# A convolution-attention and MLP-mixer kernel on one core: the order of its prologue, the queue that fetches the weights, and how chunk 0 enters the main loop

## The chip, the cores and the metric

The kernel runs on one core of a Trainium2 chip. The metric is the time of one execution on the device in microseconds (us), the median of several runs. The engines of the core work in parallel and meet at semaphores: TensorE (PE, with its weight load PEld), VectorE (DVE), ScalarE (ACT), GpSimd (POOL) and SyncE (SP). DMAs are issued by SP, ACT or GpSimd and are carried out by 16 DMA engines which the core's queues share.

## The reference

x is [8, 4096, 192], the weight generator [8, 4096, 8, 7] (both float32); the four MLP weights come as 64-bit floats. Cut to what matters:

```python
w = softmax(weight_gen, axis=-1)               # 7 taps for each of 8 heads
x = sum over k of w[..., k] * x[s - 6 + k]     # causal convolution attention
xt = x.transpose(0, 2, 1)
h = np.maximum(xt @ w_tok1, 0.0) @ w_tok2      # tokens mixed: 4096 -> 256 -> 4096
u = x + h.transpose(0, 2, 1)
h2 = np.maximum(u @ w_ch1, 0.0) @ w_ch2        # channels mixed: 192 -> 1536 -> 192
return (u + h2).astype(np.float32)
```

## The kernel before, in words

The 8 x 4096 tokens are cut into 64 chunks of 512, eight to a batch. Since w_tok1 sums over all tokens of a batch, the attention of a whole batch has to be done before the first u of that batch. Products run with two-part operands (hi and lo, fp32r), so that each product costs two or three passes.

**Prologue** (lines 914 to 1034, pools `pro` and `ps_pro`). It makes the attention of batch 0's eight chunks in 16 half chunks i: DVE multiplies the taps (`product`, L356, into `prk`, three buffers), PE adds the seven taps by 21 transposes into `tapsum` (`sums`, L362), ACT copies the sum out (`keep_sum`, L378, "the eviction"), PE turns it back (`turn_back`), ACT copies that (`keep_turned`, L393, into `xa`), and PE adds the half chunk's share of x w_tok1 into `th` (`token1_half`, L957, one half behind). Beside it the 64-bit weights are turned into float32 (`convert`, L151): each raw tile of 1024 or 768 pairs takes three ACT steps (L168, L171, L172) and one DVE step (L167). Eight such tiles are w_tok1 (`tok`), one is w_tok2's first (`w2`), three are w_ch1's thirds (`w1`), and after them comes w_ch2's first third (`c2`). The tables `loads`, `steps` and `after` say at which i a load is issued, which ACT steps stand ahead of that i's eviction (up to three), and which DVE step is put in. All loads and the stores `s0` of converted w_tok1 (`store_val`, L961) are issued by SP; only the stores `xs` of attended chunks are issued by GpSimd. Three buffers `raw` hold fetched weights, five `val` in `pro` hold converted w_tok1 until it has been stored.

**Into the main loop.** `make_h1` relus `th` into `h1`. Tiles of the pool `late` (`uf`, `u_hi`, `u_lo`, `h` and others) take the memory of `pro`. For chunk 0, `token2` makes h1 w_tok2 in PSUM (`acc`, L571), six more products (L1051) run on PE, DVE adds x into `uf` (L583, L584), and `u_parts` writes u_hi and u_lo by eight ACT casts and two DVE steps. Two rows of batch 1's first softmax stand ahead of that on DVE (L199, L200).

**Main loop, chunk g** (from L1131). `channel1(g, p)`, p = 0..5: 18 products u w_ch1 into `ph` (L637; three PSUM buffers). `take_h`: ACT relu (L643) and DVE rest (L644) into `h` (four buffers). `channel2(g, p)`: ten products h w_ch2 into `acc` (L655), and behind p = 2 the ten products of the next chunk's u (`token2`, L571, into `up`, which ACT first fills with x, L563 or L565). Everything else (conversions left over, the attention of later batches, output copies) is put between by the planner `pump`, which keeps a modelled time for each engine. In chunk 0 it has to place w_ch2's second third ahead of p = 2, its last third ahead of p = 4, and w_tok2's second tile ahead of chunk 1's u.

## Time and profile before

| | |
|---|---|
| median of 3 runs | 2085.78 us (2084.53 to 2088.27) |
| the profiled execution | 2085.23 us, of which the span of the profile is 2083.5 us |
| PE busy | 2041.8 us, 98% of the span |
| DVE, ACT, POOL busy | 1501.5, 1435.4 and 163.3 us |
| granted clock of PE, mean | 0.996 of full speed |

The profile is of one execution. Times in it are counted from the start of the span. A row of a timeline gives the idle time ahead of it and what ended it; that name is inferred from semaphores, and where a wait has several semaphores it may be another one.

### The profile page before, as it was taken

What the parts mean: (1) busy time and instruction counts of PE and PEld (TensorE: products, weight loads), DVE (VectorE), ACT (ScalarE), POOL (GpSimd) and SP (SyncE); (2) the same over time, 40 slices, a digit from 0 to 9 for tenths busy, and PEclk for the clock granted to TensorE, in tenths of its full rate; (3) what the DMA queues carried; (4) which work ended last, traced back from release to release, by engine and by line L of the source; (5) the groups of instructions that cost most, each with busy time, mean ns of one, the idle gap of its engine ahead of it and who ended that gap; (6) DMA issues with size and microseconds to landing.
All of it is one profiled execution on the core that took longest, in us unless ns stands there. A gap on an engine that the chain in (4) does not pass through costs nothing.

```text
span 2083.5 us, 32275 instructions
## 1 busy us (share of the span) xinstructions
PE 2041.8 (98%) x12832; PEld 1679.5 (81%) x12832; DVE 1501.5 (72%) x1724; ACT 1435.4 (69%) x2221; POOL 163.3 (8%) x200
## 2 busy tenths in 40 slices
PE   7799999999999999999999999999999999999998
PEld 6678888888887888888888888888888888888887
DVE  8779887888887777777777778677677765343343
ACT  6678765677766766766766766766676676676665
POOL 0000111111111000111000011010011100000000
PEclk9999999999999999999999999999999999999999
DMA  9947668788777667666656766566766654322121
GB/s 356 315 155 237 175 186 235 188 231 234 201 207 216 178 173 204 180 186 168 169 172 198 207 168 190 160 174 180 206 179 182 168 162 116 91 72 63 48 60 24
DMA packets 169815, 365.41 MB, mean 175 GB/s; under 512 B 16840, under 2 KB 110792, under 8 KB 154304
## 3 DMA queue, kind: packets, MB, share of 16 engines
q1 hardware_dynamic: 143680, 285.74, 42.6%
q0 software_dynamic: 25984, 77.61, 18.8%
q8 instruction: 101, 1.65, 0.3%
q14 instruction: 50, 0.41, 0.1%
HBM read 225.92 MB, written 71.30 MB: 143 GB/s over the span
## 4 chain that ended last, share of the span: by engine, by line
PE 78%; DVE 3%; DMA 1%; ACT 0%; issue 0%; ACTq 0%; SPq 0%; DVEq 0%
PE acc L655 35%; PE ph L637 31%; PE up L571 7%; PE th L531 4%; PE th L533 2%; DVE h L644 1%; DVE pr L231 1%; PE acc L672 0%; DMA out_dram<-out_tile 0%; DVE pr L245 0%; DMA xt<-in_x_dram 0%; ACT up L565 0%; DVE oc L712 0%; DVE xa L231 0%; DVE oa L709 0%
## 5 line engine op out<-in xcount | busy, mean ns | idle before, releaser
L655 PE MATMUL acc<-h,w2s 128*128 128x512 f32 x3800 | 886.1, 390 | 2.0 <-DVE w2s L494 2.0
L655 PEld LDWEIGHTS acc<-h,w2s 128*128 128x128 f32 x3800 | 710.4, 188 | 148.6 <-DVE w2s L494 2.4
L643 ACT ACTIVATE h<-ph 128x1024 fp32r<-128x1024 f32 x384 | 394.6, 1028 | 348.7 <-PE ph L637 302.5
L644 DVE SCALAR_TENSOR_TENSOR h<-ph,h 128x1024 fp32r<-128x1024 f32 x384 | 468.3, 1220 | 120.8 <-ACT h L643 120.1
L637 PE MATMUL ph<-u_hi,w_hi 64*128 64x512 f32 x2304 | 339.5, 395 | 7.9 <-ACT u_hi L607 4.8
L637 PE MATMUL ph<-u_lo,w_hi 64*128 64x512 f32 x2304 | 331.1, 388 | 0.6 <-ACT u_lo L612 0.3
L637 PE MATMUL ph<-u_hi,w_lo 64*128 64x512 f32 x2304 | 329.2, 387 | 0.0
L231 DVE TENSOR_TENSOR pr<-xt,wg 128x768 f32<-128x768 f32 x336 | 311.7, 947 | 0.2
L637 PEld LDWEIGHTS ph<-u_hi,w_hi 64*128 64x128 f32 x2304 | 215.1, 185 | 74.5 <-issue 19.4
L637 PEld LDWEIGHTS ph<-u_lo,w_hi 64*128 64x128 f32 x2304 | 219.9, 184 | 48.5 <-ACT u_lo L613 0.9
L637 PEld LDWEIGHTS ph<-u_hi,w_lo 64*128 64x128 f32 x2304 | 219.3, 184 | 46.9
L249 POOL DMA_DIRECT2D xa<-pr x168 | 146.5, 872 | 1408.2 <-DVE pr L245 843.6
L719 ACT COPY out_tile<-oa 32x256 f32<-32x256 f32 x504 | 203.5, 404 | 8.0
L584 DVE TENSOR_TENSOR uf<-up,uf 64x512 f32<-64x512 f32 x63 | 43.0, 683 | 211.9 <-ACT uf L579 211.9
L245 DVE TENSOR_TENSOR pr<-pr 128x768 f32<-128x768 f32 x168 | 160.2, 954 | 3.5
L571 PE MATMUL up<-w,h 128*128 128x512 f32 x630 | 160.9, 401 | 1.6 <-ACT up L565 1.2
L571 PEld LDWEIGHTS up<-w,h 128*128 128x128 f32 x630 | 114.2, 188 | 42.8 <-issue 13.4
L531 PE MATMUL th<-xh,w 128*128 128x384 f32 x384 | 112.5, 358 | 0.0
L290 DVE TENSOR_TENSOR xh<-xa,xh 128x768 fp32r<-128x768 f32 x48 | 45.8, 954 | 91.4 <-ACT xh L287 91.3
L719 ACT COPY out_tile<-oc 32x256 f32<-32x256 f32 x252 | 101.6, 403 | 7.6 <-DVE oc L712 3.1
L565 ACT COPY up<-xb 128x1024 f32<-128x1024 f32 x56 | 57.0, 1017 | 67.2 <-DVE h L644 65.8
L533 PE MATMUL th<-xh,w 128*128 128x192 f32 x384 | 96.2, 250 | 0.0
(89 smaller groups left out, 1636.4 us busy)
## 6 DMA issues: line engine op xcount, KB each, us to landing
w<-s SPq DMA_DIRECT2D x96, 1024.0 KB, 5.9
xa<-pr POOLq DMA_DIRECT2D x168, 384.0 KB, 5.0
xt<-in_x_dram SPq DMA_DIRECT2D x56, 960.0 KB, 8.1
out_dram<-out_tile SPq DMA_DIRECT2D x128, 192.0 KB, 4.7
xb<-xs SPq DMA_DIRECT2D x368, 64.0 KB, 5.3
xs<-t SPq DMA_DIRECT2D x56, 384.0 KB, 4.9
raw<-in_moe_w_tok_dram SPq DMA_DIRECT2D x16, 1024.0 KB, 12.7
s<-w POOLq DMA_DIRECT2D x8, 1024.0 KB, 5.9
```

The lines of the kernel that those rows point to most:

```text
L231: nc.vector.tensor_mul(t.rearrange("p t (h g) -> p (t h) g", h=H).rearrange("p (o n) g -> p o n g", o=1), x_k, w)
L245: nc.vector.tensor_add(sums[m], sums[m], prt.pop(m))
L249: nc.gpsimd.dma_start(xat[m].rearrange("p t d -> p (t d)"), sums[m].rearrange("p t d -> p (t d)"), accum_op=ALU.add)
L531: nc.tensor.matmul(th[:, r, 0:2 * D], w[:, c, 0, rs], xh[:, c, :], start=i + c == 0, stop=False, skip_group_check=True)
L533: nc.tensor.matmul(th[:, r, 0:D], w[:, c, 1, rs], xh[:, c, 0:D], start=False, stop=c == CT - 1, skip_group_check=True)
L565: nc.scalar.copy(up.rearrange("p k (n b c) -> p (k n) c b", c=CT, b=Q), xb.rearrange("p k (n c b) -> p (k n) c b", c=CT, b=Q))
L571: nc.tensor.matmul(up[:, n, :], h1[:, k, d], w[:, l, k * N:(k + 1) * N], start=k == 0 and j == 0 and not seeded, stop=k == KR - 1 and j == ...
L637: nc.tensor.matmul(ph[:, j, :], w[rows, k, p * P:(p + 1) * P], u[rows, k], start=n == 0, stop=n == len(steps) - 1)
L643: nc.scalar.activation(h[:, :, 0, :], ph, AF.Relu)
L644: nc.vector.scalar_tensor_tensor(h[:, :, 1, :], ph, 0.0, h[:, :, 0, :].bitcast(F32), op0=ALU.max, op1=ALU.subtract)
L655: nc.tensor.matmul(acc[:, n, :], w2s[:, f, d], h[:, j, l, :], start=False, stop=f == NF - 1 and i == len(steps) - 1, skip_group_check=True)
L719: nc.scalar.copy(dst, src[to:to + Q].rearrange("p (n e d) -> p n e d", n=2, d=Q)[:, n])
```

## The change

- **Queues.** Inside the prologue the weights are fetched by GpSimd, and `store_val` is issued by GpSimd too. SP keeps x, `xs` reads and the weight generator, whose first pair of loads goes to ACT's queue. x of chunk 0 is issued first; the two memsets of `xb` on GpSimd move behind the identity.
- **First softmax in halves.** `softmax` takes the chunks it does; chunk 0's half stands ahead of the first product and chunk 1's between the first products.
- **Order of the conversions.** Instead of `steps` there are `before` (at most two ACT steps ahead of an eviction) and `behind` (one step behind it), each starting one or two halves later; `halves` puts `token1_half` of i = 0 at 2 and of 1 and 2 at 3. The rest of w_ch1's conversion goes behind the loop. w_ch2's first and second thirds are fetched in the prologue and converted in the main loop, as is all of batch 1's softmax; the loads of batch 1's x go into the table.
- **Chunk 0's u.** PSUM tile `up` (pool `ps_acc`) is opened by eight transposes of the identity, ACT writes x into it (`seed_up`), `first_token2` adds the products, and u is split straight from PSUM (`first_u`: seven ACT and five DVE instructions). The same tile is then `acc` of chunk 0, without `seed` (a copy, L700). Two more products stand in for the six.
- **Chunk 0's first products.** `first_channel1` does p = 0 and 1 together, sorted by the third k of u's rows: for each k first the products with u_hi, then those with u_lo.
- **Planner.** `jobs` and `soon` hold the moved conversions, w_ch2's first third is asked for ahead of p = 0, and the modelled times at the start differ.

```diff
-        if pro is not None and n % 3 == 0:
+        if pro is not None and n % 3 == 0 and tag is None:
...
-        nc.sync.dma_start(
+        nc.gpsimd.dma_start(
             raw[:, 0:CT * R, :].rearrange("p n l -> p (n l)"),
...
-        nc.sync.dma_start(
+        (nc.sync if pro is None else nc.gpsimd).dma_start(
             raw[:, 0:KR * N, :].rearrange("p (k n) l -> p k (n l)", k=KR),
...
+        queue = nc.sync if pro is None else nc.gpsimd
...
+    def first_u(up):
...
+        act(hi[:, 0], up[:, 0])
+        act(hi[c, 1], up[e, 0])
+        act(hi[e, 1], up[c, 0])
+        dve.tensor_sub(lo[:, 0], up[:, 0], hi[:, 0].bitcast(F32))
+        dve.tensor_copy(uc[c], up[e, 1])
+        dve.tensor_add(uc[c], up[c, 1], uc[c])
+        act(hi[c, 2], uc[c])
+        dve.tensor_copy(hi[e, 2], uc[c])
+        act(lo[c, 1], f[e, 0])
+        act(lo[e, 1], f[c, 0])
+        dve.tensor_sub(lo[c, 2], uc[c], hi[c, 2].bitcast(F32))
+        act(lo[e, 2], f[c, 2])
+        ut[0] = hi, lo
...
+    def first_channel1(ps):
...
+        for k in range(3):
+            for steps in (((w1_hi, u_hi), (w1_lo, u_hi)), ((w1_hi, u_lo),)):
+                for p in ps:
+                    for w, u in steps:
+                        for j in range(2):
...
+        load_x(0)
+        load_wg(0, nc.scalar)
...
         def store_val(m):
-            nc.sync.dma_start(s0[m], vals[m][0])
+            nc.gpsimd.dma_start(s0[m], vals[m][0])
...
-        run(soft[0])
...
+        run(islice(soft[0], 7))
...
+        dve(w2)
+        act(w2)
+        rest(w1[0])
+        dve(w1[1])
         keep_turned(i)
+        act(w1[1])
         dve(w2)
         rest(w2)
+        dve(w1[1])
+        rest(w1[1])
+        seed_up(0, up, xbt.pop(0))
         token1_half(i)
-        rest(w1[1])
-        load_pair(NCH)
+        dve(w1[2])
...
-        rest(c2)
-        soft = softmaxes()
-        run(islice(soft, 2, 4))
...
+    first_token2(up)
+    acc_t[0] = up
+    first_u(up)
...
-            if g == 0 and p % (NP // 3) == 0 and p > 0:
+            if g == 0 and p % (NP // 3) == 0:
```

Three places of the order follow; the names are tiles, a number behind one tells buffers apart, and the line numbers of the change are its own.

GpSimd at the end of the prologue, before: the last attended chunks go out, then the store of w_tok2's first tile, the pad rows of batch 1's x, and the clearing of `uf`.

```order
L398 DMA xs5_656<-sum_603 128x768
L398 DMA xs6_755<-sum_696 128x768
L398 DMA xs7_848<-sum_789 128x768
L453 DMA s3_77<-w2_858 128x2048
L93 MEMSET xt_869 2x1152
L1045 MEMSET uf_908 64x512
```

The same place in the change: L475 fetches w_ch2's thirds, L1010 stores converted w_tok1 (`s0`) out of `val`.

```order
L398 DMA xs6_785<-sum_727 128x768
L92 MEMSET xt_787 2x1152
L475 DMA raw_793<-in_moe_w_ch2_dram 128x4x384
L1010 DMA s0_76<-val_391 128x1024
L475 DMA raw_836<-in_moe_w_ch2_dram 128x4x384
L1010 DMA s0_76<-val_438 128x1024
L398 DMA xs7_874<-sum_825 128x768
L1010 DMA s0_76<-val_570 128x1024
L1010 DMA s0_76<-val_619 128x1024
L1010 DMA s0_76<-val_724 128x1024
L453 DMA s3_78<-w2_882 128x2048
L1116 MEMSET uf_915 64x512
```

What moved: five stores out of `pro`'s `val` tiles, which SP issued before, stand on GpSimd behind fetches, and the last three of them behind the last attended chunk `xs7`.

ACT from the end of the loop to the first cast of chunk 0's u, before, with what each waits for (DMAHW is a DMA of SP's or ACT's queue, DMASW one of GpSimd's).

```order
L393 COPY xa<-turn 128x384 [waits PE_49]
L186 CAST w_858<-val 128x1024 [waits DVE_49]
L186 CAST w_hi<-val 128x3x256 [waits DVE_49]
L508 ACTIVATE h_877<-th 128x2x192 [waits PE_49]
L186 CAST w_hi<-val 128x3x256 [waits DVE_49]
L168 ACTIVATE few<-raw 128x768 [waits DMAHW3_49,DMASW5_49]
L171 ACTIVATE few<-raw 128x768 [waits Activation_49]
L172 ACTIVATE val<-raw 128x768
L493 CAST w2s<-val 128x4x192 [waits DVE_49]
L607 CAST u_hi<-uf 128x512 [waits DMAHW2_49,DMAHW3_49,DMAHW0_49,DMAHW4_49,DVE_49,Activation_49]
```

The same place in the change.

```order
L378 COPY sum<-tapsum 128x384 [waits PE_49]
L185 CAST w_882<-val 128x1024 [waits DVE_49]
L393 COPY xa<-turn 128x384 [waits PE_49]
L185 CAST w_hi<-val 128x3x256 [waits DVE_49]
L577 COPY acc<-xb_74 128x2x4x128 [waits DMAHW5_49,DMAHW6_49,DMAHW4_49,DMAHW7_49,DMAHW3_49,Pool_49]
L509 ACTIVATE h_900<-th 128x2x192 [waits PE_49]
L185 CAST w_hi<-val 128x3x256 [waits DVE_49]
L601 CAST u_hi<-acc 128x512 [waits DMASW4_49,DMASW3_49,DMASW6_49,DMASW2_49,DMAHW0_49,DMASW0_49,DMAHW1_49,PE_49,Activation_49]
L602 CAST u_hi<-acc 64x512
L603 CAST u_hi<-acc 64x512
```

What moved: the relu into h1 (L508, now L509) stands behind one w_ch1 cast as before, w_ch2's third (L168 to L493) is gone from here, x is written into PSUM ahead of the relu, and the first cast of u waits for five semaphores of GpSimd's queue, which are those of the last five stores into `s0`.

ACT in chunk 0, before, from the third relu to the filling of chunk 1's `up` with x (L563); `raw_852` is w_tok2's second tile.

```order
L643 ACTIVATE h_1027<-ph_1008 128x2x512
L700 COPY acc_1030<-uf_908 128x1024
L643 ACTIVATE h_1051<-ph_1032 128x2x512
L493 CAST w2s_70<-val_954 128x4x192
L168 ACTIVATE few_1007<-raw_852 128x1024
L172 ACTIVATE val_1006<-raw_852 128x1024
L643 ACTIVATE h_1112<-ph_1054 128x2x512
L186 CAST w2_1111<-val_1006 128x1024
L563 COPY up_1130<-xb1_72 128x2x4x128
```

In the change, from the cast of w_ch2's first third (L494) to the same filling (L577); `raw_836` is w_ch2's second third, `raw_1082` w_tok2's second tile, `raw_1117` w_ch2's last third.

```order
L494 CAST w2s_73<-val_950 128x4x192
L167 ACTIVATE few_1088<-raw_836 128x768
L171 ACTIVATE val_1087<-raw_836 128x768
L686 ACTIVATE h_1103<-ph_1041 128x2x512
L686 ACTIVATE h_1121<-ph_1060 128x2x512
L494 CAST w2s_73<-val_1087 128x4x192
L167 ACTIVATE few_1120<-raw_1082 128x1024
L171 ACTIVATE val_1119<-raw_1082 128x1024
L185 CAST w2_1143<-val_1119 128x1024
L167 ACTIVATE few_1148<-raw_1117 128x768
L171 ACTIVATE val_1147<-raw_1117 128x768
L577 COPY up_1151<-xb1_75 128x2x4x128
```

What moved: behind the cast of w_ch2's first third there now stand a whole third more and the first steps of the last third ahead of the filling of `up`.

## Rows read from the trace of the kernel before

**Rows 1.** The page of the profile, part 1: busy time of each engine, its share of the span, and its instructions.
```profile
PE 2041.8 (98%) x12832; PEld 1679.5 (81%) x12832; DVE 1501.5 (72%) x1724; ACT 1435.4 (69%) x2221; POOL 163.3 (8%) x200
```

**Rows 2.** The waits of TensorE (PE) from 138 us to the end of the span, the two longest of seven: waiting instruction, what it waited for, us in total, times, longest us.
```profile
PE ph L637 <- DVE h L644: 2.2, 1, 2.2
PE up L571 <- ACT up L565: 1.2, 2, 0.6
```

**Rows 3.** The timeline of PE at the end of the prologue and in chunk 0: start us, length us, engine, line, operation, tiles, shapes, count [idle before and what ended it].
```profile
81.07 2.46 PE L362 MATMUL tapsum<-ident,prk 128*128 128x128 f32 x21
...
85.72 1.57 PE L957 MATMUL th<-xa,val 128*128 128x192 f32 x8 [0.57 <-ACT xa L393]
...
91.28 3.86 PE L571 MATMUL acc<-w,h 128*128 128x512 f32 x10 [3.99 <-DVE h L510]
...
101.35 3.36 PE L637 MATMUL ph<-u_hi,w_hi 64*128 64x512 f32 x6 [4.83 <-ACT u_hi L607]
...
117.72 7.12 PE L655 MATMUL acc<-h,w2s 128*128 128x512 f32 x30
...
124.68 2.43 PE L571 MATMUL up<-w,h 128*128 128x512 f32 x10
...
131.34 6.44 PE L655 MATMUL acc<-h,w2s 128*128 128x512 f32 x20 [1.97 <-DVE w2s L494]
...
137.71 0.97 PE L637 MATMUL ph<-u_hi,w_hi 64*128 64x512 f32 x6
```

**Rows 4.** The timeline of VectorE (DVE), the same columns.
```profile
7.88 2.96 DVE L356 TENSOR_TENSOR prk<-xt,wg 128x2688 f32<-128x2688 f32 x1 [0.26 <-DMA xt<-in_x_dram]
...
16.86 1.23 DVE L167 SCALAR_TENSOR_TENSOR val<-val,few 128x1024 uint32<-128x1024 uint32 x1 [1.18 <-ACT val L172]
...
70.52 5.82 DVE L356 TENSOR_TENSOR prk<-xt,wg 128x2688 f32<-128x2688 f32 x2
...
99.55 2.15 DVE L583 TENSOR_TENSOR uf<-acc,xb 128x512 f32<-128x512 f32 x2
```

**Rows 5.** The timeline of ScalarE (ACT), the same columns.
```profile
83.56 0.48 ACT L378 COPY sum<-tapsum 128x384 f32<-128x384 f32 x1 [1.81 <-PE tapsum L362]
...
89.52 0.48 ACT L508 ACTIVATE h<-th 128x384 fp32r<-128x384 f32 x1
...
100.68 0.62 ACT L607 CAST u_hi<-uf 128x512 fp32r<-128x512 f32 x1 [3.29 <-DVE uf L583]
```

**Rows 6.** The timeline of GpSimd (POOL), one row: the clearing of the tile `uf` after the prologue.
```profile
98.07 0.52 POOL L1045 MEMSET uf<- 64x512 f32 x1 [8.33 <-DMA xt<-in_x_dram]
```

**Rows 7.** The instructions of line 961, the stores into `s0`, up to 130 us: durations in ns (min/median/max), first and last start us, and the time from issue to landing.
```profile
L961 SPq DMA_DIRECT2D s<-val x8: 332/428/755, 27.3 to 84.8; - x8
...
DMA to landing us min/median/max: 13.0/13.0/13.0
```

**Rows 8.** The same of line 398, the stores of attention chunks that GpSimd issues.
```profile
L398 POOL DMA_DIRECT2D xs<-sum x8: 542/542/723, 21.4 to 84.3; - x8
...
DMA to landing us min/median/max: 3.3/7.0/7.8
```

**Rows 9.** The head of the DMA view for three windows, in this order: 0 to 12 us, 12 to 60 us, and 0 to 98.1 us.
```profile
DMA packets 1140, 3.36 MB, mean 280 GB/s; under 512 B 131, under 2 KB 643, under 8 KB 1009
...
DMA packets 4234, 18.35 MB, mean 382 GB/s; under 512 B 491, under 2 KB 1771, under 8 KB 3340
...
DMA packets 11940, 33.38 MB, mean 340 GB/s; under 512 B 1246, under 2 KB 7390, under 8 KB 10781
```

**Rows 10.** Two windows: for each engine busy us and (instructions), then the granted clock of PE, the busy share of the 16 DMA engines, GB/s.
```profile
60.00:65.00 5.00, 5.00 (x45) 4.98 (x43) 5.00 (x4) 3.81 (x6) 0.00 (x0) 1.00 0.81 276
90.00:95.00 5.00, 3.72 (x11) 3.02 (x12) 2.96 (x5) 2.94 (x4) 0.00 (x0) 0.66 1.02 425
```

**Rows 11.** Three windows of 2 us, the same columns; the third number from the end is the clock (1.00 is 2.4 GHz, 0.50 is 1.2 GHz).
```profile
104.00:106.00 2.00, 2.00 (x11) 1.61 (x12) 0.00 (x0) 1.64 (x3) 0.00 (x0) 0.50 0.61 131
...
132.00:134.00 2.00, 2.00 (x6) 1.52 (x6) 1.97 (x5) 1.95 (x4) 0.00 (x0) 0.50 0.99 399
...
134.00:136.00 2.00, 2.00 (x8) 1.56 (x7) 1.21 (x2) 1.98 (x3) 0.00 (x0) 0.73 1.04 270
```

**Rows 12.** The groups of instructions by line and shape from 7 to 77 us: count | busy us, mean ns of one | idle before, one row.
```profile
L356 DVE TENSOR_TENSOR prk<-xt,wg 128x2688 f32<-128x2688 f32 x16 | 47.2, 2952 | 0.3 <-DMA xt<-in_x_dram 0.3
```

**Rows 13.** The same view from 100 to 140 us: the steps of chunk 0 and of the conversions beside it.
```profile
L644 DVE SCALAR_TENSOR_TENSOR h<-ph,h 128x1024 fp32r<-128x1024 f32 x6 | 7.2, 1222 | 7.3 <-ACT h L643 7.3
...
L643 ACT ACTIVATE h<-ph 128x1024 fp32r<-128x1024 f32 x6 | 6.2, 1028 | 5.3 <-PE acc L655 2.8 <-PE ph L637 2.4
...
L167 DVE SCALAR_TENSOR_TENSOR val<-val,few 128x1024 uint32<-128x1024 uint32 x2 | 2.5, 1226 | 0.7 <-ACT val L172 0.6
...
L168 ACT ACTIVATE few<-raw 128x1024 uint32<-128x1024 uint32 x2 | 2.3, 1158 | 0.0
...
L167 DVE SCALAR_TENSOR_TENSOR val<-val,few 128x768 uint32<-128x768 uint32 x2 | 1.9, 954 | 0.3 <-ACT val L172 0.3
...
L168 ACT ACTIVATE few<-raw 128x768 uint32<-128x768 uint32 x2 | 1.8, 895 | 0.0
...
L493 ACT CAST w2s<-val 128x768 fp32r<-128x768 f32 x2 | 1.7, 828 | 1.6 <-DVE val L176 1.6
...
L563 ACT COPY up<-xb 128x1024 f32<-128x1024 f32 x1 | 1.0, 1017 | 0.0
...
L494 DVE TENSOR_TENSOR w2s<-val,w2s 128x256 fp32r<-128x256 f32 x2 | 0.8, 420 | 0.9 <-ACT w2s L493 0.9
```

More of the change, by code (lines that the diff above doesn't have):

```diff
@@ L70, in mixer_kernel @@
     xb_, uf_ = [const.tile([P, 2, N], F32, name=f"xb{j}") for j in range(2)], []
-    for j in range(2):
-        nc.gpsimd.memset(xb_[j][0:DC, 1, :], 0.0)
     s0 = dram.tile([NCH, P, CT * R], F32, name="s0")
@@ L190, in mixer_kernel, with softmax @@
     wnt = {}
-    def softmax(m):
-        t = wgt.pop(m)
-        nt = SM * CT
-        mx = p1.tile([P, nt, H], F32, tag="mx", name="mx")
-        for j in range(SM):
-            wnt[m + j] = (t, j)
+    def softmax(m, js=range(SM)):
+        whole = wgt[m]
+        nt = len(js) * CT
+        t = whole[:, js[0] * CT:js[0] * CT + nt]
+        mx = p1.tile([P, SM * CT, H], F32, tag="mx", name="mx")[:, 0:nt]
+        for j in js:
+            wnt[m + j] = (whole, j)
         bc = lambda a: a.rearrange("p t (h o) -> p t h o", o=1).broadcast_to([P, nt, H, K])
@@ L571, in token2 @@
                     nc.tensor.matmul(up[:, n, :], h1[:, k, d], w[:, l, k * N:(k + 1) * N],
-                                     start=k == 0 and j == 0 and not seeded,
-                                     stop=k == KR - 1 and j == len(steps) - 1, skip_group_check=True)
+                                     start=False, stop=k == KR - 1 and j == len(steps) - 1, skip_group_check=True)
         yield
@@ L638, in channel1 @@
                                  stop=n == len(steps) - 1)
+        return ph
+    def first_channel1(ps):
+        u_hi, u_lo = ut[0]
+        ph = {p: ps_w.tile([P, 2, 512], F32, tag="w", name="ph") for p in ps}
+        for k in range(3):
[3 more added lines that the diff above has]
+                        for j in range(2):
+                            rows = slice(j * DC, (j + 1) * DC)
+                            nc.tensor.matmul(ph[p][:, j, :], w[rows, k, p * P:(p + 1) * P], u[rows, k],
+                                             start=k == 0 and w is w1_hi and u is u_hi, stop=k == 2 and u is u_lo)
         return ph
@@ L919, in mixer_kernel @@
         nc.scalar.activation(warm, ident[:, 0:1], AF.Exp)
-        load_wg(0)
-        load_x(0)
+        for j in range(2):
+            nc.gpsimd.memset(xb_[j][0:DC, 1, :], 0.0)
         th = ps_pro.tile([P, 2, 512], F32, tag="th", name="th")
+        up = ps_acc.tile([P, 2, 512], F32, tag="acc", name="acc")
+        for n in range(2):
+            for j in range(512 // P):
+                transpose(up[:, n, j * P:(j + 1) * P], ident, j == 0)
         jobs, vals = {}, {}
@@ new lines, in mixer_kernel @@
+        behind = {1: [(tok[0], 1)], 2: [(tok[1], 1)], 4: [(tok[2], 1)], 6: [(tok[4], 1)], 7: [(w1[0], 1)],
+                  9: [(tok[5], 1)], 10: [(tok[6], 1)], 11: [(w2, 1)], 12: [(tok[7], 1)], 13: [(w1[1], 1)],
+                  14: [(w1[2], 1)]}
+        after = {2: [tok[0]], 3: [tok[1]], 4: [tok[2]], 6: [tok[3]], 8: [tok[4]], 10: [tok[5]], 11: [tok[6]],
+                 12: [w1[0]], 13: [tok[7]]}
+        halves = {2: [0], 3: [1, 2]}
+        def load(what):
+            if isinstance(what, int):
+                load_x(what)
+            elif what[0] == "s":
+                store_val(int(what[1:]))
+            elif what[:2] == "xb":
+                load_xt(int(what[2:]))
+            elif what[:2] == "wg":
+                load_wg(int(what[2:]))
+            elif what[:2] == "c2":
+                fetch_channel("c2", int(what[2:]), ("raw", "w1")[int(what[2:])])
@@ L1015, in mixer_kernel @@
                 keep_turned(i - 1)
-            for what, n in steps[i]:
+            for what, n in before.get(i, ()):
+                if n:
+                    act(what, n)
+            keep_sum(i)
+            for j in halves.get(i, range(i - 1, i) if i > 3 else ()):
+                token1_half(j)
+            turn_back(i)
+            for what, n in behind.get(i, ()):
                 act(what, n)
-            keep_sum(i)
-            if i > 0:
-                token1_half(i - 1)
-            turn_back(i)
             if i % 2 == 1:
                 store_sum(i // 2)
-            for what in loads[i]:
+            for what in loads.get(i, ()):
                 load(what)
+            for what in fetches.get(i, ()):
+                load(what)
+        dve(w2)
+        act(w2)
+        rest(w1[0])
+        dve(w1[1])
         keep_turned(i)
+        act(w1[1])
         dve(w2)
         rest(w2)
+        dve(w1[1])
+        rest(w1[1])
+        seed_up(0, up, xbt.pop(0))
         token1_half(i)
-        rest(w1[1])
-        load_pair(NCH)
+        dve(w1[2])
+        spare = ps_pro.tile([P, 512], F32, tag="turn", name="turn", bufs=2)
+        for _ in range(2):
+            nc.tensor.matmul(spare, w1_hi[:, 0, 0:P], w1_hi[:, 0, 0:512], start=True, stop=True)
         make_h1(0, th[:, :, 0:D])
+        act(w1[2])
         rest(w1[2])
-        rest(c2)
-        soft = softmaxes()
-        run(islice(soft, 2, 4))
-        state["jobs"] = deque([(convert_channel, "c2", 2)] + [(convert_w2, i) for i in range(2, NCH)])
+        x_at[NCH] = LOAD
+        state["vals"] = 0
         pro = None
-        state["vals"] = 0
     late = ctx.enter_context(tc.tile_pool(name="late", bufs=1))
-    ps_acc = ctx.enter_context(tc.tile_pool(name="ps_acc", bufs=1, space=bass.MemoryType.PSUM))
     ps_w = ctx.enter_context(tc.tile_pool(name="ps_w", bufs=3, space=bass.MemoryType.PSUM))
```

129 lines of the change are left out of this document (63 added, 66 removed).

## The prediction

> **What bounds the kernel now.** I read the page first: PE is busy 98% of the span [rows 1]. Then PE's waits from 138 us on: the longest row is 2.2 us in total [rows 2], so behind chunk 0 the main loop runs on PE without a gap that matters. Chunk 0 ends at 137.7 us, where chunk 1's first products start [rows 3]. The change leaves those 1946 us alone, so it is worth what it moves that instant, no more. Next the timelines ahead of it. DVE multiplies from 7.9 us to 76.3 us with one stop of 1.2 us [rows 4]; 16 multiplications of 2.95 us are 47 us of that [rows 12]. PE adds the last half chunk only at 81.1 us [rows 3], because the evictions on ACT ran late behind three conversion steps. The first cast of chunk 0's u is at 100.7 us [rows 5], 24.3 us behind the last multiplication, and the first product of the main loop at 101.35 us, after 4.8 us of idle PE [rows 3].
>
> What ended that wait? GpSimd cleared `uf` at 98.07 us after waiting 8.3 us for a DMA [rows 6]. The profile names a load of x, but `uf` lies in memory of the prologue's pool, whose last reader is the last store into `s0`: issued at 84.8 us, with 13.0 us to landing [rows 7], that is 98.1 us. DVE came to the add at 99.55 us [rows 4]. So u is held by two things within 1.5 us of each other, the DMA queue and DVE, and both have to move. In the change the first cast of u waits for these stores itself (the second place of the order).
>
> **The change part by part.**
>
> *Start of the loop.* x of chunk 0 is issued first, but its second piece still waits for DVE's memset of the pad rows, so I take 0.4 us off the first multiplication (bounds 0 and 1). The stop of 1.2 us goes, since the first conversion is wanted later; w_ch1's low part, a step like the 0.95 us row of 768 columns [rows 13], moves behind the loop. Against that, chunk 1's half softmax comes between the first products: about 1.5 us. The last multiplication ends at 76.3 - 0.4 - 1.2 - 0.9 + 1.5 = 75.3 us. The ACT steps that are moved lie beside DVE's multiplications, as before, and cost nothing while DVE is the slower one; with at most two ahead of an eviction PE should now be on time.
>
> *Loop to u.* With T = 75.3: 21 transposes 2.5 us [rows 3], share of the half before 1.5, eviction 0.5 beside it [rows 5], turn 0.5, copy 0.5, share 1.6 [rows 3], relu 0.5 [rows 5], ten products at the full clock 2.4 (the row at 124.68) [rows 3]: T + 9.8 with the hops, so the operands of u are there at 85.1 us instead of 95.1. DVE's conversions in between (w_tok2's shift, three w_ch1 steps, each 1.0 to 1.2 us [rows 13]) end in time for the relu's low part, within 0.5 us. DVE's two adds of x (2.15 us) [rows 4] and the two softmax rows are off this path; x's copy into PSUM (1.02 us) [rows 13] lies ahead of the relu while PE still works.
>
> *The stores.* They stand on GpSimd behind the fetches, and the last three behind the last attended chunk, whose copy is ready at T + 3.1 = 78.4 us. Four issues of 0.54 us follow [rows 8], so the last leaves at 80.6 us; with 3.3 to 7.0 us to landing [rows 8] it lands at 83.9 to 87.6 us if the queue ahead of it is short. It isn't. By the tiles' sizes 32.5 MB have to go ahead of it: ten x loads 9.8, w_tok1 and w_tok2's first tile 9.4, w_ch1 2.4, two thirds of w_ch2 1.6, weight generator 1.2, `xs` out 3.1 and back 0.8, `s0` 4.2. Before, 33.4 MB had moved by 98.1 us [rows 9]. With 3.4 MB by 12 us, the rest at the 382 GB/s of 12 to 60 us lands at 88.2 us; at the 340 GB/s of the whole stretch [rows 9] everything lands at 95.5 us. The ends for u are thus 86.5 us (short queue) and 95.5 us. I take **90 us**, near the row of 12 to 60 us: two rings that are both full should avoid stretches like 60 to 65 us, where the engines were busy 0.81 of the time, and with stores on one ring and loads on the other they moved 425 GB/s at 90 to 95 us [rows 10]; 1.8 us are left for small packets. u then comes 10.7 us earlier than at 100.7.
>
> *Chunk 0.* Count from the first cast of u. Before, w_ch2's products start at +17.0, chunk 1's u products at +24.0, and chunk 0 ends at +37.0 [rows 3]. PE idles from about 85 to 90 us in the change, and after 4.8 idle us the clock was at its lower level (0.50) until about 107 us [rows 11]; so the first 36 products (18 pairs, run side by side in half the rows) take until +7.5 by the same loss, in spite of the sorting, which lets PE start on the first third of u. Then it goes by ACT and DVE. Four relus of 1.03 us with one conversion step between, held by the three PSUM buffers, end at +13.0 on ACT and +14.2 on DVE. Now w_ch2's *first* third has to be converted here: ACT step 0.9, two DVE steps 0.95, cast 0.83, low part 0.42 [rows 13]: products start at +17.5, as before. The second third: two ACT steps to +18.6, a DVE step to +19.6; its other DVE step stands behind the fourth h (which needs p = 0 done at +19.8) and ends at +23.0, cast +23.9, behind h of p = 5 the low part at +24.8. p = 1 was done at +22.0: PE stands 2.7 us. w_tok2's second tile is fetched when the first third is converted, lands in time, and takes two ACT steps of 1.13, two DVE steps of 1.23, a cast and a low part: +30.9; two steps of the last third stand ahead of `up`'s filling [rows 13], which ends at **+32.1**, where it was +23 before. PE has done p = 2 by +28.9 and stands another 3.2 us. Each such stop brings the lower clock: the one of 1.97 us did, for about 3.5 us [rows 3, 11], 1.8 us of loss. Ten products to +36.1 and three times 2.3 give +43.0 for +37.0. Bounds: +41.0 (no cold start, one stop less) and +44.5.
>
> *Nothing to count:* the copy `seed` of chunk 0 (1.02 us of ACT), six warming products for two, and batch 1's softmax, which the loop hides behind 98% PE. The moved work is as much as before relative to chunk 0's end.
>
> **The sum.** 90.0 - 100.7 + (43.0 - 37.0) = -4.7 us. On the profiled execution's 2085.2 us, 0.55 us under the median and inside its runs, this makes 2080.5 us. The measurement can tell about 0.2%, 4.2 us, from no change.
>
> **The rivals.**
>
> *The stores don't bind.* If the rings empty faster, u starts at 86.5 us with PE still at the higher clock, chunk 0 ends at +41.8, and the gain is 14.2 - 4.8 = 9.4 us: 2075.8 us. For it: 425 GB/s when both rings held work [rows 10]. Against it: five stores are issued in the last 8 us. Chance 0.22.
>
> *DMA is no faster than before.* 32.5 MB at 340 GB/s: u at 95.5 us, -5.2 + 6.0 = +0.8 us, 2086 us. For it: the engines were busy at nearly all times [rows 10], and who issues doesn't alter the bytes. The Trainium skill ("DMA: Bandwidth & Descriptors", Rules for kernel authors) says that spreading DMAs over SP, ACT and GpSimd brings no bandwidth, as all run on the same 16 engines; by that rule this rival is the forecast, and the trace agrees only for stretches at full busy share. Chance 0.22.
>
> *GpSimd's queue becomes the bound* (the slow side). 45 DMAs are issued there ahead of u. At 0.54 us [rows 8] they take 24 us of some 70. If each had to wait out half a multiplication of DVE (1.5 us) [rows 12], they take 92 us from about 7 us on, the last store leaves near 99 us and lands at 104: u at 104.5, +3.8 + 6.0 = +9.8 us, 2095 us. It decides from about 1.5 us a DMA on. Against it: eight issues beside a DVE that never paused took 0.54 to 0.72 us [rows 8]. The Trainium skill ("SBUF — State Buffer", SBUF: two separate sides) warns that GpSimd cannot write DMA descriptors while DVE runs in a two-port mode and that such DMAs seem blocked; by that rule the price is this one, and the rows of before don't show it. Chance 0.06.
>
> *The evictions stay late.* If waiting raw tiles hold ACT, PE adds the last half at 81 us as before, the last store leaves at 86 and lands at 92.3 us: -8.4 + 6.0 = -2.4 us, 2082.8 us. Chance 0.05.
>
> **How the numbers follow.** The forecast (u at 88 to 93 us) has 0.45 and reaches from 2078 to 2084. Faster by over 0.2%: 0.22 of the first rival and 0.28 of the forecast, 0.50. Within: 0.17 of the forecast, 0.20 of the second, 0.04 of the last, 0.41. Slower: 0.09. The range for 8 in 10 goes from 2073.5 (short queue, +41) to 2088.5 (u at 95.5 us, +44.5, some waits later).
>
> **What would show it.** Right: the last multiplication near 75 us, the last transposes right behind it; the first cast of u held by a DMA until about 90 us with PE idle and then at 1.2 GHz; stops of PE ahead of w_ch2's second third and of chunk 1's u, and chunk 0 some 43 us long. Wrong: u cast right behind its products (first rival); GpSimd issues of over 1 us each (third); chunk 0 no longer than 37 us, which would add 6 us to the gain; new waits of PE behind chunk 0.

## The result, and the profile after

The changed kernel takes 2097.64 us (median of 4 runs, 2096.75 to 2098.8) against 2087.03 us for the kernel before on the same chip: ratio 1.0053, 95% interval 1.0035 to 1.007. It is **slower by about 0.5%**, where 0.25% faster was forecast. The profiled execution took 2096.75 us, its span is 2095.0 us, 11.5 us more than before.

PE on the page, the counterpart of [rows 1], tells nothing of it:

```profile
PE 2043.4 (98%) x12836; PEld 1680.5 (80%) x12836; DVE 1502.5 (72%) x1731; ACT 1432.9 (68%) x2220; POOL 182.3 (9%) x237
```

The timeline of PE around chunk 0, for [rows 3]:

```profile
99.71 2.56 PE L590 MATMUL acc<-w,h 128*128 128x512 f32 x10
109.62 0.79 PE L680 MATMUL ph<-u_hi,w_hi 64*128 64x512 f32 x2 [7.35 <-ACT u_hi L601]
...
127.28 4.83 PE L698 MATMUL acc<-h,w2s 128*128 128x512 f32 x20 [1.48 <-DVE w2s L495]
134.87 3.89 PE L698 MATMUL acc<-h,w2s 128*128 128x512 f32 x10 [2.76 <-DVE w2s L495]
142.15 4.13 PE L566 MATMUL up<-w,h 128*128 128x512 f32 x10 [3.39 <-ACT up L577]
146.13 7.04 PE L698 MATMUL acc<-h,w2s 128*128 128x512 f32 x30
153.09 0.97 PE L666 MATMUL ph<-u_hi,w_hi 64*128 64x512 f32 x6
```

Chunk 0 ends at 153.09 us, 15.4 us later than before (137.71). The first cast of u is at 108.98 us and was at 100.68: 8.3 us. From there to chunk 1's first product it is 44.1 us for 37.0, with three stops of PE: another 7.1 us. Behind chunk 0 the kernel needs 1941.9 us for 1945.8, so 3.9 us come back.

The timeline of DVE, for [rows 4], with its long stops:

```profile
11.54 2.96 DVE L356 TENSOR_TENSOR prk<-xt,wg 128x2688 f32<-128x2688 f32 x1 [4.35 <-DMA xt<-in_x_dram]
...
40.19 1.23 DVE L166 SCALAR_TENSOR_TENSOR val<-val,few 128x1024 uint32<-128x1024 uint32 x1 [4.05 <-ACT val L171]
...
73.89 1.23 DVE L166 SCALAR_TENSOR_TENSOR val<-val,few 128x1024 uint32<-128x1024 uint32 x1 [3.78 <-ACT val L171]
...
83.43 5.82 DVE L356 TENSOR_TENSOR prk<-xt,wg 128x2688 f32<-128x2688 f32 x2
```

The first multiplication starts 3.7 us later than before. The last ends at 83.43 + 5.82 = 89.25 us for 76.34. The timeline of ACT, for [rows 5], says what is behind two of these stops and what held u:

```profile
36.18 0.58 ACT L201 ACTIVATE wg<-wg 128x448 f32<-128x448 f32 x1 [2.23 <-DVE wg L200]
36.67 1.14 ACT L167 ACTIVATE few<-raw 128x1024 uint32<-128x1024 uint32 x1
...
72.73 1.12 ACT L171 ACTIVATE val<-raw 128x1024 f32<-128x1024 f32 x1 [3.81 <-DMA s<-val]
...
108.98 0.58 ACT L601 CAST u_hi<-acc 128x512 fp32r<-128x512 f32 x1 [8.01 <-DMA s<-val]
```

At 36.18 us ACT stood for an exponential that needs DVE, with the third tile's conversion queued behind it; then DVE stood for that conversion. At 72.73 us a conversion wanted a `val` buffer whose store had left at 61 us and not landed. At 108.98 us u waited 8.0 us for the last stores.

GpSimd's own timeline, its waits up to 115 us (waiting instruction, what for, us in total, times, longest) and the stores into `s0` (durations in ns, first and last start, time to landing, as [rows 7]):

```profile
2.19 1.77 POOL L405 DMA_DIRECT2D raw<-in_moe_w_tok_dram  x3
...
34.25 0.55 POOL L398 DMA_DIRECT2D xs<-sum  x1 [6.74 <-ACT sum L378]
34.79 0.53 POOL L405 DMA_DIRECT2D raw<-in_moe_w_tok_dram  x1
...
56.61 0.55 POOL L398 DMA_DIRECT2D xs<-sum  x1 [7.27 <-ACT sum L378]
57.14 0.54 POOL L1010 DMA_DIRECT2D s<-val  x1
57.68 0.54 POOL L405 DMA_DIRECT2D raw<-in_moe_w_tok_dram  x1
```

```profile
POOL xs L398 <- ACT sum L378: 44.9, 7, 19.6
```

```profile
L1010 POOL DMA_DIRECT2D s<-val x8: 532/540/564, 57.1 to 97.8; - x8
...
DMA to landing us min/median/max: 4.3/10.3/11.8
```

GpSimd stood 44.9 us for evictions, ahead of stores of attended chunks (L398), and fetches (L405) and stores (L1010) left right behind these stores. The issues themselves stay at 0.54 us. The first store into `s0` left at 57.1 us (27.3 before), the last at 97.8 (84.8 before). The DMA engines moved less meanwhile; the head of the DMA view for 12 to 60 us (its first row is the busy share of the DMA engines, in tenths, in 40 slices) and for 0 to 109 us, for [rows 9]:

```profile
DMA  9999999992430489697997942679885969479589
...
DMA packets 3026, 13.65 MB, mean 284 GB/s; under 512 B 432, under 2 KB 1200, under 8 KB 2433
...
DMA packets 9945, 33.39 MB, mean 306 GB/s; under 512 B 1294, under 2 KB 4588, under 8 KB 8842
```

284 GB/s where it was 382, with stretches in which the engines were nearly idle; the same 33.4 MB that had gone by 98.1 us went by 109 us. **What makes fetches and stores leave late** is the question for the experiments.

### The profile page after: what moved, and what is told of

Same layout as the page of the kernel before. It is cut to its first block, busy times and chain, and to the rows that moved or that the text cites. A ratio compares the mean times of both kernels' runs of the same rounds, so it can differ in the third digit from the quotient of the medians.

```text
span 2095.0 us, 32295 instructions
## 1 busy us (share of the span) xinstructions
PE 2043.4 (98%) x12836; PEld 1680.5 (80%) x12836; DVE 1502.5 (72%) x1731; ACT 1432.9 (68%) x2220; POOL 182.3 (9%) x237
## 4 chain that ended last, share of the span: by engine, by line
PE 80%; DVE 2%; ACT 0%; issue 0%; ACTq 0%
PE acc L698 36%; PE ph L666 32%; PE up L566 7%; PE th L532 4%; PE th L534 2%; DVE h L687 1%; DVE pr L231 1%; PE acc L715 0%; DVE pr L245 0%; ACT up L579 0%; DVE oc L755 0%; DVE w L186 0%; ACT h L686 0%; DVE oa L731 0%; DVE t L312 0%
## 5 line engine op out<-in xcount | busy, mean ns | idle before, releaser
L666 PE MATMUL ph<-u_hi,w_hi 64*128 64x512 f32 x2292 | 333.7, 393 | 0.9 <-ACT u_hi L649 0.6
L534 PE MATMUL th<-xh,w 128*128 128x192 f32 x384 | 96.2, 250 | 0.0
```

What stands on the lines that cost most here:

```text
L534: nc.tensor.matmul(th[:, r, 0:D], w[:, c, 1, rs], xh[:, c, 0:D], start=False, stop=c == CT - 1, skip_group_check=True)
L666: nc.tensor.matmul(ph[:, j, :], w[rows, k, p * P:(p + 1) * P], u[rows, k], start=n == 0, stop=n == len(steps) - 1)
```

## The experiments

Each was timed beside the kernel before on its chip (2085.3 to 2086.5 us in the four sessions); the ratio and its 95% interval are to that, over all runs of both, so they can differ a little from the quotient of two medians. "Loop" is the end of DVE's last multiplication, "u" the first cast of chunk 0's u, "end" chunk 1's first product.

### One order at a time, in the changed kernel

Stores as early as their tile is ready (e1):

```diff
-        fetches = {2: [tok[3]], 3: [tok[4]], 4: [w1[0]], 6: [tok[5]], 7: ["s0", tok[6]], 8: [w2, "s1"], 9: [tok[7]],
-                   10: ["s2", w1[1]], 11: [w1[2]], 13: ["c20", "s3"], 14: ["c21", "s4"], 15: ["s5", "s6", "s7"]}
+        fetches = {2: [tok[3], "s0"], 3: [tok[4], "s1"], 4: [w1[0], "s2"], 6: [tok[5], "s3"], 7: [tok[6]], 8: [w2, "s4"],
+                   9: [tok[7]], 10: [w1[1], "s5"], 11: [w1[2], "s6"], 13: ["c20", "s7"], 14: ["c21"]}
```

> The change with its eight stores of converted w_tok1 issued by GpSimd in the half chunk in which the tile is converted (0 to 5 half chunks earlier), nothing else moved. Theory 'late stores': in the changed kernel the store of the second tile left at 61 us and held ACT for 3.8 us (and DVE behind it), and the last stores left at 96.7 to 98.3 us and held the first cast of u for 8.0 us. Both stops go; the last multiplication ends near 85 us, u is cast near 98 us (its products end at 102.3 in the change, 4 us earlier here), chunk 0 ends at about 142 us: 2086 us, bounds 2084 and 2090. Rival 'GpSimd DMAs are slow in themselves': the same bytes in the same queue land as late (10 us each), and u waits for them still: 2094 to 2098 us.

Measured: 2091.0 us (ratio 1.0027, 1.0016 to 1.0037), just above the bounds of the first theory: about half of the change's loss is gone. u is cast at 101.8 us and waits for its products alone, so the 8.0 us wait is gone. But the loop still ends at 89.2 us: DVE's stop of 3.78 us became one of 4.88 us, behind a fetch that landed late (rows of ACT, then of DVE):

```profile
78.37 1.12 ACT L167 ACTIVATE few<-raw 128x1024 uint32<-128x1024 uint32 x1 [3.74 <-DMA raw<-in_moe_w_tok_dram]
...
101.79 0.58 ACT L601 CAST u_hi<-acc 128x512 fp32r<-128x512 f32 x1 [1.38 <-PE acc L590]
```

```profile
82.25 1.22 DVE L166 SCALAR_TENSOR_TENSOR val<-val,few 128x1024 uint32<-128x1024 uint32 x1 [4.88 <-ACT val L171]
```

Half of the theory held (u's wait); the other stop was only handed on.

Everything on SP in the same place of the program (e2), then only the first three fetches on SP (e3):

```diff
-            nc.gpsimd.dma_start(s0[m], vals[m][0])
+            nc.sync.dma_start(s0[m], vals[m][0])
...
-        queue = nc.sync if pro is None else nc.gpsimd
+        queue = nc.sync
```

```diff
-        nc.gpsimd.dma_start(
+        (nc.sync if i < 3 else nc.gpsimd).dma_start(
             raw[:, 0:CT * R, :].rearrange("p n l -> p (n l)"),
```

> The change with all prologue fetches of weights and all stores of converted w_tok1 back on SP, in the same place of the program. Theory 'order, not queue': the first x gets ahead of the weights (first multiplication at 8 instead of 11.5 us), but the 4.0 us stop of DVE at 36 us (an order of ACT's steps) and the late stores stay: 2090 us, bounds 2087 to 2096. Rival 'GpSimd DMAs are slow in themselves': all of the 12.8 us that the loop lost against the kernel before and the wait for the stores go: 2083 us or less.

> The change with only the first three fetches of w_tok1 on SP, behind the loads of x there; all others stay on GpSimd. Theory 'the first x shares the DMA engines with 3 MB of weights': the first multiplication starts at 8 to 8.5 instead of 11.5 us and everything behind it comes 2 to 3.5 us earlier: 2094 to 2096 us. Rival 'the first x is late for another reason (the memset of the pad rows ahead of it)': still 11.5 us, 2097.6 us.

Measured: e2 2096.64 us (1.0054, 1.0039 to 1.0069): no gain at all, outside both expectations. The loop ends 5 us earlier (84.2), yet u is cast at 109.3 after a wait of 14.4 us. On SP the last three stores left at 92.5 to 94.1 us, and GpSimd's clearing of `uf`, which reuses the memory that they read, waited for them until 109.3, some 15 us after the last one left (rows of ACT, then of POOL; the row of ACT names another DMA for the same instant):

```profile
109.29 0.59 ACT L601 CAST u_hi<-acc 128x512 fp32r<-128x512 f32 x1 [14.38 <-DMA xb<-xs]
...
109.33 0.52 POOL L1116 MEMSET uf<- 64x512 f32 x1 [16.48 <-DMA s<-val]
```

e3 2095.55 us (1.0049, 1.0034 to 1.0064): the first multiplication starts at 8.1 us as foretold, the loop ends 3.1 us earlier, u, which waits 8.9 us for stores, comes 2.0 us earlier, and chunk 0, 1.1 us longer here, ends 0.9 us earlier. So the first x did share the engines with 3 MB of weights, though it was issued ahead of them on SP.

The third tile's ACT steps ahead of the exponential (e4):

```diff
-        behind = {1: [(tok[0], 1)], 2: [(tok[1], 1)], 4: [(tok[2], 1)], 6: [(tok[4], 1)], 7: [(w1[0], 1)],
+        behind = {1: [(tok[0], 1)], 2: [(tok[1], 1)], 3: [(tok[2], 3)], 6: [(tok[4], 1)], 7: [(w1[0], 1)],
```

> The change with the three ACT steps of w_tok1's third tile put ahead of the exponential of the third softmax on ACT. Theory 'order of ACT's steps': DVE's stop of 4.05 us at 36 to 40 us falls to 1.5 us or less and the loop ends 2.5 us earlier: 2095 us. Rival 'it is given back': the next stops (fetches that wait on GpSimd, the store at 61 us) take it over, 2097.6 us within 0.5 us.

Measured: 2094.9 us (1.0044, 1.0027 to 1.006). DVE's stop falls from 4.05 to 1.31 us and the loop ends 3.1 us earlier; u still waits 9.2 us, and is 2.2 us earlier. All three edits together (e5):

> The change with the three edits at once: stores of converted w_tok1 as early as their tile is ready, the first three fetches on SP behind x, the third tile's ACT steps ahead of the exponential. Theory 'three separate waits': apart, these gave 6.6, 2.0 and 2.7 us, so 2086 us together, u cast at 96 to 98 us. Rival 'the DMA engines' bytes decide': with the loop's own waits gone, the next fetch of w_tok1 (it landed at 78.4 us with the early stores alone) takes them over, u is cast at 100 to 102 us as with the early stores alone: 2090 to 2091 us.

Measured: 2085.58 us (0.9996, 0.9987 to 1.0006), the first theory. Loop 83.0, u 96.2, end 140.6 us. The three orders together cost about what the change lost; without them it equals the kernel before.

### Tables and queue, two by two

e6 gives the changed kernel the tables of the kernel before; e10 that and SP; e8 is the kernel before with GpSimd's queue.

```diff
-        before = {1: [(tok[0], 0)], 2: [(tok[0], 2)], 3: [(tok[1], 2)], 4: [(tok[2], 2)], 5: [(tok[3], 2)],
...
+        before = {0: [(tok[0], 3)], 1: [(tok[1], 2)], 2: [(tok[1], 1), (tok[2], 1)], 3: [(tok[2], 2)],
...
+        behind = {}
```

> The change with the tables of the kernel before for the prologue's loop (which conversion step stands ahead of which eviction, which fetch and store is issued at which half chunk); queues, u from PSUM, the softmax in halves, w_ch2's thirds in the main loop and the sorted products stay as in the change. Theory 'conversions that start later free the three raw tiles later, so fetches leave later and the DMA engines stand idle at 20 to 60 us': they move 370 GB/s or more in 20 to 60 us (225 to 314 in the change), the last multiplication ends at 80 us or earlier, the last store lands at 98 to 101 us, u is cast there, and with a chunk 0 of 44 us this makes 2085 to 2089 us. Rival 'the queue is it': GpSimd's fetches stand behind the stores of attended chunks whatever the tables, and the loop ends at 86 us or later: 2093 to 2097 us.

> The change with the tables of the kernel before and with SP for the prologue's fetches and stores, that is, both edits that did little alone (2096.6 us with SP alone, 2095.8 with the tables alone). Theory 'either one makes the last stores late': with both, DVE multiplies without stops as in the kernel before, the last multiplication ends at 77 us, the last store lands at 96 to 99 us and u is cast there; with a chunk 0 of 44 us: 2084 to 2087 us. Rival 'the loads of batch 1's x, which SP has to wait for ahead of the last stores, hold them': u at 103 us or later, 2091 us or more.

> The kernel before with its prologue's fetches of weights and stores of converted w_tok1 issued by GpSimd instead of SP, nothing else changed. Theory 'the queue itself does little': only the first x comes later behind the first fetches (first multiplication at 9 to 11.5 instead of 7.9 us); since u waits for the last store, chunk 0 ends 0 to 3.5 us later: 2085 to 2089 us. Rival 'fetches by GpSimd are slow, or wait behind its stores of attended chunks': the loop stretches by 8 us or more: 2093 us or more.

| tables of | queue | us | ratio | loop | u |
|---|---|---|---|---|---|
| the change | GpSimd (the change) | 2097.64 | 1.0053 | 89.3 | 109.0 |
| the change | SP (e2) | 2096.64 | 1.0054 | 84.2 | 109.3 |
| before | GpSimd (e6) | 2095.77 | 1.0048 (1.0031 to 1.0064) | 83.0 | 107.4 |
| before | SP (e10) | 2088.41 | 1.0008 (0.9999 to 1.0017) | 77.0 | 100.6 |
| before, kernel before | GpSimd (e8) | 2099.36 | 1.0063 (1.0048 to 1.0078) | 85.6 | 113.0 |

Either one, new tables or GpSimd's queue, is enough to bring u to 107 us or later; only without both is it at 100.6 (and there too it waits 9.8 us for the last stores, more than I expected of e10, whose time lies between its theory and its rival). The loop's end itself adds up: against 89.3 us it comes 5.0 us earlier without the queue, 6.3 without the new tables and 12.3 without both. What hides is u, which goes by the last landing: with the queue alone undone, the stores hold it for 14.4 us. That is why e2 showed nothing, and e6 little (its time is that of its rival). And e8 **refuted my theory that the queue does little**: alone, it costs the kernel before 13 us. The row of ACT in e10:

```profile
100.58 0.58 ACT L601 CAST u_hi<-acc 128x512 fp32r<-128x512 f32 x1 [9.80 <-DMA s<-val]
```

### What in the queue

In e8 GpSimd waited 50.3 us for evictions, and w_tok1's eighth tile was fetched behind such a wait, at 66.06 us instead of 51.29 (rows of POOL):

```profile
65.52 0.55 POOL L398 DMA_DIRECT2D xs<-sum  x1 [11.80 <-ACT sum L378]
66.06 0.53 POOL L405 DMA_DIRECT2D raw<-in_moe_w_tok_dram  x1
```

e13 takes that order away (ACT, which makes the attended chunks, issues their stores), e14 puts the first three fetches on SP, e15 does both; fetches and stores of weights stay on GpSimd.

```diff
-        nc.gpsimd.dma_start(xst[m], sumt.pop(m))
+        nc.scalar.dma_start(xst[m], sumt.pop(m))
```

> The kernel before with fetches and stores of converted weights on GpSimd (2099.4 us), and the eight stores of attended chunks issued by ACT, which makes them, instead of GpSimd. Theory 'fetches wait in GpSimd's order behind stores that wait for an eviction' (GpSimd waited 50.3 us for evictions there): w_tok1's eighth tile is fetched at 55 us instead of 66, the loop's stops behind 60 us go, the last store leaves near 90 us, u is cast at 104 to 106 instead of 113.0 us: 2090 to 2093 us. Rival 'DMAs that GpSimd issues are slow in themselves': nothing changes by more than 1.5 us, 2098 us or more.

> The kernel before with fetches and stores of converted weights on GpSimd, but the first three fetches of w_tok1 on SP behind and between the loads of x and of the weight generator, as in the kernel before. Theory 'three tiles at once at 2 us hold up the first x, the weight generator and the first tile itself': first multiplication at 8 instead of 11.2 us, first conversion step at 13.4 instead of 18.4 us, everything 4 to 5 us earlier: 2094 to 2095.5 us. Rival 'given back at the fetches that wait behind stores': 2098 us or more.

> Both of these edits on the kernel before with GpSimd's fetches and stores. Theory 'these two orders are all that the queue costs': back at the kernel before, 2085 to 2088 us. Rival 'a part of it is GpSimd itself': 2091 us or more.

Measured: e13 2088.29 us (1.0018, 1.0009 to 1.0028), e14 2093.3 (1.0035, 1.0021 to 1.0049), e15 2085.39 (0.9996, 0.9986 to 1.0005); the first two are a little below what their theories gave. In the traces u, cast at 113.0 us in e8, comes at 104.8, 109.0 and 99.5 us (100.7 in the kernel before). So these two orders make up the queue's 13 us: with both gone, the core's DMAs moved 398 GB/s in 12 to 60 us (e8: 336), u was held by DVE, as in the kernel before, and a loss by GpSimd itself is at most 1 us by the interval (rows: the DMA view of e15, then ACT):

```profile
DMA packets 4602, 19.12 MB, mean 398 GB/s; under 512 B 544, under 2 KB 1576, under 8 KB 3704
```

```profile
99.54 0.62 ACT L607 CAST u_hi<-uf 128x512 fp32r<-128x512 f32 x1 [3.30 <-DVE uf L583]
```

The end of chunk 0 (150.3 us in e8; 139.6, 145.8 and 134.4 here) says less: in e13 and e15 the clock stayed at 1.00 behind the stop of 1.97 us that brought it to 0.50 in the kernel before [rows 11], so that the 20 products behind it took 4.8 to 4.9 us for 6.4: most of the 2.2 us by which chunk 0 is shorter there. No run tells why. The window behind that stop in e15, columns as in [rows 11]:

```profile
130.00:132.00 2.00, 2.00 (x10) 1.67 (x9) 1.97 (x6) 1.93 (x4) 0.00 (x0) 1.00 0.89 338
```

The stores of attended chunks were not moved to ACT in the changed kernel; there, only the first three fetches were moved (e3, e5). GpSimd's waits in e15 up to 110 us are mostly for free raw tiles, as they should be, and the weights leave in time (timeline):

```profile
POOL raw L405 <- ACT val L172: 32.8, 5, 14.8
```

```profile
46.68 0.53 POOL L405 DMA_DIRECT2D raw<-in_moe_w_tok_dram  x1 [3.81 <-ACT val L172]
```

The eighth tile now leaves at 46.7 us.

### Chunk 0, and a version that is faster

e7 converts w_ch2's first third where ACT and DVE stand for u; e9 also fetches w_tok2's second tile there. From e9's edit; of these lines e7 has the first alone:

```diff
         rest(w1[2])
+        rest(("c2", 0))
+        fetch_w2(1, "raw")
...
-    state["jobs"] = deque([(convert_w2, 1), (convert_channel, "c2", 2)] + [(convert_w2, i) for i in range(2, NCH)])
+    state["jobs"] = deque([(convert_channel, "c2", 2)] + [(convert_w2, i) for i in range(2, NCH)])
```

> The change with w_ch2's first third converted ahead of the first cast of u, where ACT and DVE stand for 8 us. Theory 'chunk 0 is longer by the conversions that moved into it': from the first cast of u to chunk 1's first product 37 to 39 us instead of 44.1, the stops of PE ahead of the first and the second third of w_ch2 (1.5 and 2.8 us) and most of that ahead of chunk 1's u (3.4 us) go, u's cast stays at 109 us: 2091 to 2092.5 us. Rival 'the fill of chunk 1's u is late anyway, by w_tok2's second tile': its stop grows by what the others give back, 2095 us or more.

> As the run that converted w_ch2's first third ahead of u, and w_tok2's second tile is fetched right behind it instead of in the main loop, so that the three tiles that chunk 0 converts are fetched as early as in the kernel before. Theory 'chunk 0 is longer by what is fetched and converted in it': from the first cast of u to chunk 1's first product 37 to 38.5 us (44.1 in the change, 37.0 in the kernel before), u cast at 107 to 109 us as in the change: 2090 to 2092 us. Rival 'it is the sorted products and u from PSUM that make chunk 0 longer': still 43 us or more, 2096 us.

Measured: e7 2102.4 us (1.0083, 1.0068 to 1.0098), slower still, and on the side of its rival: the two stops at w_ch2 are gone, but PE stands 10.65 us ahead of chunk 1's u, because the filling of `up` comes as late as in the change (140.77 us for 141.10). On ACT a step of w_ch2's last third, whose raw tile was still on its way, stands ahead of the filling of `up` (rows of ACT, then of PE):

```profile
139.21 0.89 ACT L167 ACTIVATE few<-raw 128x768 uint32<-128x768 uint32 x1 [3.53 <-DMA raw<-in_moe_w_ch_dram]
...
140.77 1.02 ACT L577 COPY up<-xb 128x1024 f32<-128x1024 f32 x1
```

```profile
141.84 4.64 PE L566 MATMUL up<-w,h 128*128 128x512 f32 x10 [10.65 <-ACT up L577]
```

That is not all of its loss: of the 4.6 us by which its span is longer than the change's, 0.8 us is there when chunk 0 ends, and 3.8 us come behind it, where a wait of PE for h (2.0 us) is back.

e9 2091.75 us (1.0027, 1.0016 to 1.0037): from u to the end 38.5 us (148.91 - 110.39) instead of 44.1. The conversions and the fetches that moved into chunk 0 are thus 5.6 of its 7.1 us, and both had to move back; the other 1.5 us I did not trace.

e11 puts together what held: u from PSUM, softmax in halves and sorted products of the change; tables and SP fetches of the kernel before; stores into `s0` by GpSimd in the half chunk after their conversion; x of batch 1 fetched behind the loop; the three ACT steps of w_ch2's first third between the relu and u, and w_tok2's second tile fetched in the prologue. e12 is e11 with chunk 0's first products unsorted (`channel1` in place of `first_channel1`).

> The change's u from PSUM, softmax in halves and sorted products, with the tables and fetches of the kernel before (SP), the stores of converted w_tok1 issued by GpSimd in the half chunk after their conversion, batch 1's x fetched behind the loop, w_ch2's first third converted between the relu and the first cast of u, and w_tok2's second tile fetched in the prologue. Theory 'the u path of the change is worth 9 to 11 us, and the queue, the late stores and the moved conversions ate it': last multiplication at 77 us, u cast at 90 to 93 us held by its own products, chunk 0 of 38 us, end of chunk 0 at 128 to 131 us for 137.7 in the kernel before: 2077 to 2080 us. Rival 'the DMA bytes decide': w_ch1's last third or a store lands late and u is cast at 97 us or later: 2084 to 2087 us.

> The combined kernel with chunk 0's first two groups of products in the order of the kernel before (by u_hi w_hi, u_hi w_lo, u_lo w_hi) instead of sorted by third. Theory 'the sorting lets PE start on the first third of u': the products start when all three thirds of u_hi are there, 2 to 3 us later, and chunk 0 ends 1 to 2.5 us later than in the combined kernel. Rival 'ACT and DVE set chunk 0's length': no difference within 0.5 us.

Measured: **e11 2077.82 us (0.9963, 0.9951 to 0.9976), faster than both kernels.** u at 94.4, end 132.85 us; PE keeps one long stop, 3.82 us, ahead of chunk 1's u. I had expected u to be held by its own products; these end at 93.0 us, and w_ch2's steps stand ahead of u on ACT until 94.3. The end of chunk 0 missed its 128 to 131 us too; the time came into its range by luck, with 3.6 us behind chunk 0 that the theory had not counted. The rows of ACT, then of PE:

```profile
93.47 0.86 ACT L171 ACTIVATE val<-raw 128x768 f32<-128x768 f32 x1
94.36 0.59 ACT L601 CAST u_hi<-acc 128x512 fp32r<-128x512 f32 x1
```

```profile
121.90 4.13 PE L566 MATMUL up<-w,h 128*128 128x512 f32 x10 [3.82 <-ACT up L577]
```

e12 2078.89 us (0.9969, 0.9958 to 0.9979): its first group of products is cut by a wait of 2.13 us, and from u to the end it takes 40.4 us for 38.5, but the two times can't be told apart, so no time shows what the sorting is worth. The row of PE in e12:

```profile
99.35 0.79 PE L666 MATMUL ph<-u_hi,w_hi 64*128 64x512 f32 x2 [2.13 <-ACT u_hi L607]
```

## Why the prediction was wrong, point by point

Against the kernel before the span grew by 11.5 us: the loop ends 12.9 us later, its end to the end of u's products takes 5.8 us less (13.0 for 18.8), from there to u 1.2 us more, chunk 0 7.1 us more, the rest 3.9 us less. Against the forecast u came 19.0 us late (108.98 for 90): 14.0 by the loop's end, 3.2 by the way from there to u's products and 1.8 by the stores behind them.

- **Where chunk 0 ends decides: right**, but for a constant. The changed kernel and all experiments made from it, e7 excepted (1945.7), need 1941.9 to 1942.3 us behind chunk 0.
- **Start of the loop, the step that failed.** Its end was forecast at 75.3 us and came at 89.25. I wrote that x of chunk 0 is issued first and took 0.4 us off: it came 3.7 us later (e3, e14). I wrote that moved ACT steps "cost nothing while DVE is the slower one": but DVE's own next step waits for them, and 8.1 us of stops more came in, half of it by one step behind an exponential (e4). By the runs of two by two, the queue is 5.0 us of the loop's delay and the tables 6.3. The changed program showed the order: three ACT steps of the third tile stand right behind it, and I read of the table only that at most two are ahead of an eviction.
- **Loop to u.** Forecast T + 9.8 us, measured 13.0: a late w_ch1 fetch held ACT ahead of the last eviction but one, so PE wasn't on time.
- **The stores.** The mechanism was right: u waited 8.0 us for the last ones, with PE idle. Their time was wrong, 108.98 us instead of 90. I took 382 GB/s because "two rings that are both full" would keep the engines busy; they moved 284 GB/s in 12 to 60 us, with idle stretches. A loop that ended in time would not have saved this term: in e10, with the stores on SP, it ends at 77.0 us, and u still waits for them until 100.58. Two slips have no bearing on the miss: 84.8 and 13.0 us make 97.8, not 98.1 (`uf` was cleared at 98.07 all the same), and the terms named for the lower end of the range (86.5, +41) give 2075.0, not 2073.5.
- **GpSimd's queue**, counted at nothing in the forecast. The third rival's time, 2095 us, came near by luck, by another mechanism than its own: not 1.5 us an issue (0.54 us measured) but fetches in order behind stores that wait for an eviction (e13) and three fetches ahead of x (e14). I had named the evictions that the last stores stand behind, and not the fetches behind the earlier ones. The Trainium skill ("SBUF — State Buffer", SBUF: two separate sides) has GpSimd's descriptors blocked beside some DVE modes; e15, with GpSimd's DMAs beside the same DVE work and no loss, doesn't show it.
- **DMA no faster than before** (the second rival): 340 GB/s was still too much, 306 GB/s. The Trainium skill's rule ("DMA: Bandwidth & Descriptors", Rules for kernel authors), that issuing from several engines brings no bandwidth, holds in e15 to within 4%: 398 GB/s with both queues, 382 with SP alone.
- **Chunk 0.** 43.0 us forecast, 44.1 measured; stops of 2.76 and 3.39 us for my 2.7 and 3.2, and one of 1.48 us that I had not. "Each such stop brings the lower clock" was too strong: behind the stop of 1.48 us the clock stayed at 1.00 (127 to 131 us), as behind the one of 1.97 us in e13 and e15. The clock behind the last stop is near its lower level, 0.53 (window, columns as in [rows 11]):

```profile
142.50:144.50 2.00, 2.00 (x7) 1.51 (x6) 1.93 (x4) 0.72 (x2) 0.00 (x0) 0.53 1.05 442
```

- **Behind chunk 0**, counted at nothing, the change gains 3.9 us. The waits of PE there (views as in [rows 2]) add up to 2.7 us for 5.8, and the 2.2 us wait for h is gone; the other 0.8 us I did not trace. The experiments made from the change keep this gain, so it is part of why e11 wins (4.9 us by the end of chunk 0, 3.6 us behind it).

The sum thus failed in its first term, u's time, by what leaves late in the prologue and by the conversions that DVE stood for. With the loop ending at 77 us and stores that don't bind, as in e11, u is 6.3 us ahead of the kernel before.
